# Attention and routed experts on one core: the first pairs' steps in another order, two experts with fewer places

## The chip, the cores and the metric

The kernel runs on 1 core of a Trainium2 chip. The metric is device time in microseconds (us) of one execution, the median over several runs. An execution's own time is a little longer than its span, which reaches from the first to the last instruction of the profiled execution.

## The reference, cut to what matters

Three layers follow one another: attention that is masked by clusters, a gated layer with a causal convolution, and eight experts of which each token visits one.

```python
def _attn_ref(q, k, v, centroids):            # 2 batches, 8 heads, 768 tokens, 64 wide, 16 clusters
    q_assign = np.argmax(np.einsum('bhsd,hcd->bhsc', q_n, c_n), axis=-1)
    k_assign = np.argmax(np.einsum('bhsd,hcd->bhsc', k_n, c_n), axis=-1)
    mask = q_assign[:, :, :, None] == k_assign[:, :, None, :]
    scores = np.where(mask, scale * np.matmul(q, k.transpose(0, 1, 3, 2)), -1000000000.0)
    attn = np.exp(scores - np.max(scores, axis=-1, keepdims=True))
    attn = attn / (np.sum(attn, axis=-1, keepdims=True) + 1e-09)
    return np.matmul(attn, v)
...
def _moe_ref(x, w_val, conv_w, w_out):        # gate: sigmoid of a causal convolution of 5 taps
    return gate * (x @ w_val) @ w_out
...
def _moe2_ref(x, w_gate, w_local, w1, w2):    # 8 experts, 512 -> 1024 -> 512
        for s in range(S):
            fresh_e = int(np.argmax(logits[b, s]))
            e = fresh_e if s == 0 or local_gate[b, s] < 0.5 else prev_e
            prev_e = e
            out[b, s] = softmax(logits[b, s])[e] * (np.maximum(x[b, s] @ w1[e], 0.0) @ w2[e])
```

How many tokens an expert gets depends on the inputs. With the inputs that the reference draws (seed 0), and after 128 tokens of the first batch's largest expert are taken out (the kernel treats them ahead of the rest), the experts hold 306, 260, 220, 203, 132, 104, 102 and 81 tokens, sorted by size. These counts were worked out by running the reference.

## The kernel before, in words

**Attention.** Eight pairs of heads follow one another (`gi` 0 to 7). For each pair, `assign` (step "bg" of the plans) finds the clusters: matmuls `sim`, then on the VectorE (DVE) a transpose `s`, a maximum `amx`, a comparison `eq`, a transpose `et`, then a matmul `bef` and a DVE operation `r` (for the first pair `rb`). `rows` sends the one-hot rows `od` by DMA into the operands `q`, `km` and `oq`. `mx_part` makes score tiles `mx` on TensorE (PE) and reduces each on DVE into `mn`; from these come row maxima, which go back into row 96 of `q`: for the first two pairs by `mx_first` (DVE `mfr`, PE `mt`, ScalarE (ACT) `q<-mt`), later by a DMA. `scores` makes each score tile with two matmuls (`s<-xq,xk`, then `s<-q,km`), ACT takes the exponential into `p`, GpSimd (POOL) sums the `p` into `acc`, and PE multiplies by `v` (`pv`). `prep`, `prep_lo` and `prep_x` split q and k into a high part (`hiq`, `hik`, on ACT) and the remainder (POOL, "qlo" and "klo") and write the operands by DMA. The weights of the next layer (`raww_val`, `raww_out`) are loaded in between and split on DVE in four operations (`split64`: `expw_val`, `topw_val`, ...); the small convolution weights `rawc` take the same way (`small`).

**What sets the order.** Nothing is scheduled by a compiler: every engine runs its instructions in the order in which the program issues them, and all DMAs of the attention are issued by one queue, SyncE's (SP), in its order. `first_pair` writes that order for pair 0 with what the next two pairs need. It counts places n from 0 to 56. At each it issues one `mx` tile, then the steps that the table `FIRST` has at this place, in the table's order, then the row maxima (`LAG`: at place 6i the DVE part of group i is made, its PE part at place 6i + LAG[i]), then as many letters of `ORDER` as `GO` lets through (l: first score matmul of a tile, s: second matmul, exponential and sum, p: `pv`, e: `pv<-oq,eh` and its copy to `xu`). `pair` does the same for pairs 1 to 5 with the table `PLAN`, whose places go from 0 to 35 in each pair, and for the last two with `LATE`, which is not changed.

The PE part of a row maximum is a `mt` matmul behind a DVE reduction:

```python
        nc.vector.tensor_reduce(out=mr, in_=self.mn[gi][:, t0:t0 + n], axis=AX.X, op=ALU.max,
                                negate=True)
        yield
        ps = self.ps_m.tile([128, 512], F32, tag="m", name=f"mt{gi}{h}{a}")
```

**The experts.** The token lists are built on the core, experts sorted by size. `CAPS` holds the places of the first, second, ... largest expert; the tokens beyond them go to blocks of 128 in `beyond`, a loop whose count is read at run time and which runs not at all where every expert fits. In `Ffn.up` (lines 1403 to 1411) an expert with n places up to 256 takes, for each of 32 weight tiles, one matmul `ph<-x,wh` with 2n columns and one `ph<-x,wl` with 256. In `Ffn.down` (line 1447) full tiles of tokens take three matmuls of 512 columns per weight tile. A last tile of 64 or 32 tokens is done otherwise (`rest`, line 1455): matmuls `po<-ws,hr` whose outputs stand beside one another on 64 or 32 partitions, with 256 or 128 columns each. A last tile of 96 is treated as a full one with fewer rows.

Of the kernel before, what the change touches and what calls it, by code (L numbers as in the profile page):

```python
# [34 lines left out]
CAPS = [320, 288, 256, 224, 192, 192, 160, 128]  # L35
# [12 lines left out]
class Attn:  # L48
# [5 lines left out]
    PLAN = (("klo", (22,)), ("acc1", (12,)), ("q", (10,)), ("rows", (21,)), ("qx", (6,)), ("mx", (1, 2, 6, 8, 8, 13, 13, 15, 17, 19, 21, 22, 29, 29, 29, 35)), ("ld", (7,)), ("bg", (3, 5, 5, 7, 7, 15, 15, 24)), ("k", (7,)), ("vs", (11,)), ("vm", (23,)), ("kx", (3,)), ("acc2", (21,)), ("row", (28,)), ("v", (4,)), ("sums", (7, 8, 8, 12, 15, 16, 17, 27, 30, 30)), ("pv", (2, 9, 11, 15, 21, 27, 30, 32, 35)), ("work", (1, 5, 6, 13, 18, 28, 31, 32)), ("qlo", (20,)), ("max", (26,)), ("acc3", (26,)), ("acc4", (31,)), ("sm", (3, 10)))  # L54
    LATE = (("row", (28,)), ("max", (19,)), ("kx", (24,)), ("mx", (1, 3, 4, 8, 8, 10, 12, 13, 13, 15, 20, 21, 21, 23, 23, 23, 23, 29, 29, 29)), ("v", (0,)), ("work", (9, 10, 12, 16, 20, 27, 27)), ("vm", (28,)), ("sums", (6, 11, 12, 16, 21, 24, 25, 27, 28)), ("acc1", (12,)), ("acc4", (35,)), ("pv", (0, 5, 11, 16, 21, 23, 28, 35)), ("acc2", (21,)), ("vs", (13,)), ("qx", (15,)), ("acc3", (22,)), ("sm", (0, 7)))
    MORE = (("mx", (2,)), ("work", (35,)))


    LAG = (7, 10, 14, 12, 28, 6, 13, 13)
    FIRST = (("bg0", (0,)), ("bg0", (0,)), ("q0", (0,)), ("qlo2", (41,)), ("bg0", (0,)), ("bg0", (0,)), ("one1", (16,)), ("bg0", (0,)), ("k2", (32,)), ("bg1", (0,)), ("k0", (0,)), ("klo0", (0,)), ("bg1", (6,)), ("qx0", (1,)), ("bg0", (0,)), ("rows1", (9,)), ("qlo0", (0,)), ("rows0", (17,)), ("v0", (0,)), ("bg1", (0,)), ("bg0", (0,)), ("kx0", (0,)), ("work", (18,)), ("bg1", (0,)), ("rest", (8,)), ("ld2", (10,)), ("klo1", (13,)), ("vs1", (42,)), ("vm1", (52,)), ("qx1", (28,)), ("bg2", (24, 25, 30, 33, 33, 40, 40, 44)), ("bg1", (0,)), ("bg1", (6,)), ("oh0", (0,)), ("v1", (26,)), ("q1", (13,)), ("qlo1", (20,)), ("kx1", (29,)), ("vm0", (16,)), ("vs0", (13,)), ("bg0", (4,)), ("bg1", (0,)), ("klo2", (42,)), ("oh1", (2,)), ("k1", (6,)), ("rows2", (55,)), ("one2", (33,)), ("ld3", (35,)), ("q2", (38,)), ("bg1", (0,)), ("work", (36, 37, 39, 40, 40, 45, 47, 50, 55)))  # L60
    ORDER = "lllsslsslslsllspsllspspplslslsplsplslslselsllssppllslplssppspe"
# [1843 lines left out]
```

## Time and profile before

| | us |
|---|---|
| median of 3 runs | 566.21 |
| the three runs | 566.21, 567.31, 560.71 |
| the profiled execution's own time | 563.89 |
| its span | 562.1 |
| first pair, from the start to pair 1's first scores | about 70 |
| pairs 1 to 7 | about 70 to 285 |
| gated layer and routing | about 285 to 380 |
| experts | about 380 to 562 |

The profile is of one execution. In its views a row gives the start, the duration, the engine, the source line, the operation with output<-input, and in brackets how long the engine stood idle before it and what released it. PEld is the weight load that goes ahead of a matmul, SPq the DMA queue of SyncE. "PEclk" or "granted clock" is TensorE's clock as a share of full speed: 1.00 is 2.4 GHz, 0.50 is 1.2 GHz. Matmuls overlap, so a duration of 0.34 us may stand in a row of matmuls that start every 0.18 us.

### The profile page before, as it was taken

To read this page: it belongs to the slowest core of one execution; us is meant where nothing else is said; L and a number is where in the kernel's file an instruction comes from. 1 tells how busy PE (TensorE), PEld (TensorE's weight loads), DVE (VectorE), ACT (ScalarE), POOL (GpSimd) and SP (SyncE) were. 2 spreads that over 40 slices of the span, in tenths; PEclk is the share of its full clock that TensorE was granted. 3 is DMA by queue.
4 is the path that set the end of the run, shared out by engine and by line. 5 is a ranking of instruction groups with operands and counts; after the bars stand their busy time and mean duration, and the time that the engine had idled before them with its cause. 6 is when DMAs were issued, how large, how long until landed. Compare 5 with 4: busy or idle time off the path is not lost. (4 is left out here: it accounts for less than half of the span.)

```text
span 562.1 us, 9334 instructions
## 1 busy us (share of the span) xinstructions
PE 522.1 (93%) x3328; PEld 387.0 (69%) x3328; DVE 387.3 (69%) x694; ACT 293.8 (52%) x569; POOL 257.9 (46%) x195
## 2 busy tenths in 40 slices
PE   3898979999998999999988999999999999999992
PEld 0564545565655665667678899859898888978892
DVE  4756768787788689767978563646737568479671
ACT  2635354554554565686464241435534548559671
POOL 4475728697897878877931010042013133022011
PEclk9998897999999999999999999999999999999997
DMA  8896284676757452200000038289364887556840
GB/s 203 216 228 184 88 219 127 172 185 169 199 153 174 120 141 81 67 12 0 1 10 0 21 108 305 94 272 342 114 205 162 281 251 232 179 182 211 295 166 14
DMA packets 53180, 86.90 MB, mean 155 GB/s; under 512 B 6313, under 2 KB 30321, under 8 KB 53132
## 3 DMA queue, kind: packets, MB, share of 16 engines
q1 hardware_dynamic: 49996, 78.36, 47.1%
q0 software_dynamic: 3136, 7.92, 4.4%
q8 instruction: 27, 0.44, 0.3%
q14 instruction: 21, 0.17, 0.1%
HBM read 59.65 MB, written 8.62 MB: 121 GB/s over the span
## 5 line engine op out<-in xcount | busy, mean ns | idle before, releaser
L307 DVE TENSOR_REDUCE mn<-mx 128x1 f32<-128x512 f32 (+1 forms) x156 | 94.3, 639 | 29.6 <-PE mx L303 29.4
L398 ACT ACTIVATE p<-s 128x384 f32<-128x384 f32 x168 | 75.4, 488 | 58.5 <-PE s L397 55.3
L1354 DVE TENSOR_TENSOR wl<-ws,wh 128x1024 fp32r<-128x1024 f32 x64 | 77.5, 1222 | 11.0 <-ACT wh L1353 9.8
L476 POOL TENSOR_TENSOR acc<-acc,p 128x768 f32<-128x768 f32 x42 | 84.4, 2033 | 0.5
L1353 ACT ACTIVATE wh<-ws 128x1024 fp32r<-128x1024 f32 x64 | 66.6, 1056 | 6.3 <-DMA ws<-in_w_dram 6.3
L396 PE MATMUL s<-xq,xk 128*128 128x384 f32 x168 | 63.9, 380 | 3.4 <-ACT p L398 3.4
L1480 POOL DMA_INDIRECT out_dram<-o,L x12 | 14.5, 1212 | 112.5 <-ACT o L1479 99.2
L492 PE MATMUL pv<-p,v 128*64 128x384 f32 x336 | 64.8, 507 | 0.0
L303 PE MATMUL mx<-km,q 80*128 80x512 f32 (+1 forms) x192 | 60.7, 387 | 2.3 <-DVE mn L307 1.9
L397 PE MATMUL s<-q,km 97*128 97x384 f32 x168 | 57.4, 342 | 0.0
L1408 PE MATMUL ph<-x,wh 128*128 128x384 f32 (+4 forms) x192 | 56.5, 338 | 0.0
L396 PEld LDWEIGHTS s<-xq,xk 128*128 128x128 f32 x168 | 32.0, 191 | 34.7 <-issue 19.2
L796 DVE SCALAR_TENSOR_TENSOR gp<-xT,cwt,gp 128x767 f32<-128x767 f32 (+3 forms) x32 | 51.5, 1625 | 2.5 <-ACT gp L790 2.1
L1411 PE MATMUL ph<-x,wl 128*128 128x256 f32 x192 | 51.6, 279 | 0.0
L303 PEld LDWEIGHTS mx<-km,q 80*128 80x128 f32 x192 | 37.3, 207 | 15.4 <-DVE mn L307 8.1
L492 PEld LDWEIGHTS pv<-p,v 128*64 128x64 f32 x336 | 20.7, 138 | 27.8 <-issue 27.4
L1447 PE MATMUL po<-wh,hh 128*128 128x512 f32 x96 | 39.0, 407 | 0.0
L1408 PEld LDWEIGHTS ph<-x,wh 128*128 128x128 f32 x192 | 36.1, 188 | 3.2 <-issue 1.0
L1447 PE MATMUL po<-wh,hl 128*128 128x512 f32 x96 | 37.8, 393 | 0.0
L1447 PE MATMUL po<-wl,hh 128*128 128x512 f32 x96 | 37.6, 391 | 0.0
L1411 PEld LDWEIGHTS ph<-x,wl 128*128 128x128 f32 x192 | 36.0, 188 | 0.1
L476 POOL TENSOR_TENSOR acc<-p,p 128x768 f32<-128x768 f32 x14 | 26.2, 1884 | 20.7 <-ACT p L398 20.7
(350 smaller groups left out, 1096.7 us busy)
## 6 DMA issues: line engine op xcount, KB each, us to landing
ws<-in_w_dram SPq DMA_DIRECT2D x72, 512.0 KB
qt<-in_qT_dram SPq DMA_DIRECT2D x8, 384.0 KB
kt<-in_kT_dram SPq DMA_DIRECT2D x8, 384.0 KB
q<-hiq SPq DMA_DIRECT2D x16, 192.0 KB
km<-hik SPq DMA_DIRECT2D x16, 192.0 KB
v<-in_v_dram SPq DMA_DIRECT2D x8, 384.0 KB
xk<-kt SPq DMA_DIRECT2D x16, 192.0 KB
xk<-hik SPq DMA_DIRECT2D x16, 192.0 KB
```

Source lines behind the costliest of these rows:

```text
L303: nc.tensor.matmul(ps[:, n * p:n * p + n], lhsT=q2[0:80, h, t * 128:t * 128 + 128], rhs=km[0:80, h, c:c + n], start=(p == 0), stop=True, s ...
L307: nc.vector.tensor_reduce(out=out, in_=src, axis=AX.X, op=ALU.max)
L396: nc.tensor.matmul(ps, lhsT=kl[:, h, ks], rhs=t1[:, h, hs], start=True, stop=False)
L397: nc.tensor.matmul(ps, lhsT=km[:97, h, ks], rhs=q2[:97, h, hs], start=False, stop=True)
L398: nc.scalar.activation(pt[:, h, hs], ps, AF.Exp, scale=1.0 / D ** 0.5)
L476: eng.tensor_tensor(t[:, h], p(0)[:, h] if first is None else t[:, h], p(j)[:, h], op=ALU.add)
L492: nc.tensor.matmul(self.pvt[64 * h:64 * h + 64, i, :HS], lhsT=v[:, j, 64 * h:64 * h + 64], rhs=pt[:, h, half(i)], start=False, stop=(j == ...
L1353: nc.scalar.activation(hi, t, AF.Copy)
L1354: nc.vector.tensor_tensor(lo, t, f32(hi), op=ALU.subtract)
L1408: nc.tensor.matmul(ps[:, m, :2 * n], lhsT=hi[:, k, ms], rhs=x[:, k, :2 * n], start=st, stop=False, skip_group_check=True)
L1411: nc.tensor.matmul(ps[:, m, :256], lhsT=lo[:, k, ms], rhs=x[:, k, :256], start=False, stop=sp, skip_group_check=True)
L1447: nc.tensor.matmul(self.po[r][i][:m], lhsT=a[:, k, ts], rhs=w[:, q], start=(k == 0 and z == 0), stop=(k == KF - 1 and z == 2))
```

## The change

The tables of the first pair (`LAG`, `FIRST`, `ORDER`, `GO`) and of pairs 1 to 5 (`PLAN`) are written anew, and two numbers of `CAPS` are smaller. The tables' other lines are not shown, since their numbers say nothing to a reader; what they do to the engines' order stands below. The `made` lines only record and assert the order while the program is built and issue nothing.

```diff
-CAPS = [320, 288, 256, 224, 192, 192, 160, 128]
+CAPS = [320, 288, 224, 224, 192, 160, 160, 128]
...
-    LAG = (7, 10, 14, 12, 28, 6, 13, 13)
...
+    LAG = (6, 10, 14, 10, 27, 6, 12, 10)
...
-    ORDER = "lllsslsslslsllspsllspspplslslsplsplslslselsllssppllslplssppspe"
...
+    ORDER = "lllsslsslslsllspsllspspplsllssplsplslslslelslssppllslplssppspe"
...
+        self.made |= {("sim", gi, "q"), ("sim", gi, "k")}
...
     def prep_lo(self, gi, which):
+        assert ("sim", gi, which) in self.made
...
+        self.made.add(("pv", 0, n))
...
-        assert self.t2
+        assert self.t2 and ("pv", 0, NT * h + NT - 1) in self.made
```

The first place is PE, in the middle of the first pair, around the row maximum of pair 1's second group (`mx_5_1`, `mt`). `s_17` to `s_19` are score tiles of pair 0, two matmuls each. Before:

```order
L423 MATMUL s_16_592<-q_0_85,km_88 128x384
L451 MATMUL pv_443<-oq_129,eh_131 64x384 x2
L413 MATMUL s_17_603<-xq_91,xk_93 128x384
L423 MATMUL s_17_603<-q_0_85,km_88 128x384
L413 MATMUL s_18_607<-xq_91,xk_93 128x384
L413 MATMUL s_19_609<-xq_91,xk_93 128x384
L423 MATMUL s_18_607<-q_0_85,km_88 128x384
L303 MATMUL mx_5_1_613<-km_89,q_1_86 128x384
L343 MATMUL mt_628<-identr,mfr_626 128x128 x3
L423 MATMUL s_19_609<-q_0_85,km_88 128x384
```

And of the changed kernel:

```order
L425 MATMUL s_16_592<-q_0_85,km_88 128x384
L415 MATMUL s_17_598<-xq_91,xk_93 128x384
L454 MATMUL pv_443<-oq_129,eh_131 64x384 x2
L305 MATMUL mx_5_1_605<-km_89,q_1_86 128x384
L345 MATMUL mt_620<-identr,mfr_618 128x128 x3
L305 MATMUL mx_6_0_625<-km_89,q_1_86 128x384
L415 MATMUL s_18_631<-xq_91,xk_93 128x384
L425 MATMUL s_17_598<-q_0_85,km_88 128x384
L305 MATMUL mx_6_1_635<-km_89,q_1_86 128x384
L305 MATMUL mx_7_0_642<-km_89,q_1_86 128x384
L415 MATMUL s_19_646<-xq_91,xk_93 128x384
L425 MATMUL s_18_631<-q_0_85,km_88 128x384
```

Four matmuls of the score tiles 17 to 19 that stood ahead of `mx_5_1` and `mt` now stand behind them; on ACT the exponentials of tiles 17 and 18 likewise move behind `q<-mt`, and `hiq` moves from behind tile 19 to ahead of tile 18.

The second place is PE at the end of the first pair. `pv_443<-oq_129,eh_131` is the last reader of `oq_129`, the buffer into which SP writes pair 2's `oq`; `vm` is a small matmul for the mean of v. Before:

```order
L343 MATMUL mt_734<-identr,mfr_685 128x128 x3
L423 MATMUL s_23_697<-q_0_85,km_88 128x384
L441 MATMUL pv_443<-p_4_594,v_202 64x384
L441 MATMUL pv_443<-p_5_689,v_202 64x384
L364 MATMUL vm_744<-vs_682,ones 64x128
L366 MATMUL vm_744<-cnt_279,selg 64x1
L343 MATMUL mt_754<-identr,mfr_539 128x128 x3
L451 MATMUL pv_443<-oq_129,eh_131 64x384 x2
```

And of the changed kernel:

```order
L345 MATMUL mt_734<-identr,mfr_685 128x128 x3
L444 MATMUL pv_443<-p_4_594,v_200 64x384
L444 MATMUL pv_443<-p_5_689,v_200 64x384
L454 MATMUL pv_443<-oq_129,eh_131 64x384 x2
L345 MATMUL mt_748<-identr,mfr_538 128x128 x3
L366 MATMUL vm_753<-vs_683,ones 64x128
L368 MATMUL vm_753<-cnt_279,selg 64x1
```

The last reader of `oq_129` now stands ahead of `vm` and of one `mt`, and `s_23` has gone further up.

The third place is DVE early in pair 1, where the weights `raww_val` are awaited from a DMA; `t_0<-sm` begins the sums of pair 0. Before:

```order
L185 TENSOR_TENSOR eq_832<-s_3_815,amx_830 128x384
L307 TENSOR_REDUCE mn_775<-mx_2_1_845 128x2
L728 TENSOR_SCALAR expw_val_850<-raww_val_834 128x512
L188 STREAM_TRANSPOSE et_860<-eq_832 128x384
L534 STREAM_TRANSPOSE t_0_870<-sm_821 128x384
```

And of the changed kernel:

```order
L186 TENSOR_TENSOR eq_832<-s_3_819,amx_830 128x384
L309 TENSOR_REDUCE mn_775<-mx_2_1_841 128x2
L189 STREAM_TRANSPOSE et_845<-eq_832 128x384
L731 TENSOR_SCALAR expw_val_852<-raww_val_834 128x512
L537 STREAM_TRANSPOSE t_0_866<-sm_821 128x384
```

`et`, which needs no DMA, moves ahead of the operation that waits for one. The same two operations change places in pairs 3 and 4 (there with `raww_out`).

Besides these: on DVE, near the start, `rb` moves ahead of the second pair's `amx`; on SP the loads of pair 2's q and k move ahead of the DMAs of pair 1's `od` rows, and in pairs 1 to 5 two `km` writes move ahead of the q and k loads; on POOL in pairs 1 to 5 the remainder of k moves ahead of the sum over `p_2`; on PE in pairs 1 to 5 one `pv` matmul group and one `mx` tile change places.

## Rows read from the trace of the kernel before

**Rows 1.** The page's first part: busy time by engine.

```profile
PE 522.1 (93%) x3328; PEld 387.0 (69%) x3328; DVE 387.3 (69%) x694; ACT 293.8 (52%) x569; POOL 257.9 (46%) x195
```

**Rows 2.** Windows: length, busy PE, PEld, DVE, ACT, POOL; then clock, DMA share, GB/s.

```profile
50.00:52.00 2.00, 0.08 (x1) 0.00 (x0) 1.75 (x7) 0.76 (x2) 1.08 (x2) 1.00 0.99 336
...
54.00:56.00 2.00, 2.00 (x7) 0.62 (x6) 1.50 (x3) 0.55 (x1) 0.89 (x1) 0.50 0.19 46
...
66.00:68.00 2.00, 1.93 (x11) 0.70 (x10) 1.56 (x4) 0.97 (x2) 1.88 (x2) 1.00 0.00 0
...
86.00:88.00 2.00, 2.00 (x8) 0.47 (x4) 1.91 (x3) 0.06 (x1) 2.00 (x3) 0.50 1.05 246
```

**Rows 3.** Timeline of 47 to 54 us: PE's first long hole and its neighbours.

```profile
49.74 0.34 PE L303 MATMUL mx<-km,q 80*128 80x384 f32 x1
...
51.96 0.15 DVE L338 TENSOR_REDUCE mfr<-mn 128x3 fp32r<-128x9 f32 x1
...
52.26 0.52 PE L343 MATMUL mt<-identr,mfr 128*128 128x128 f32 x3 [2.19 <-DVE mfr L338]
...
53.71 0.83 ACT L261 ACTIVATE hiq<-qt 128x768 fp32r<-128x768 f32 x1
```

**Rows 4.** Timeline of 73 to 83 us: PE's second long hole and what leads to it.

```profile
73.52 0.58 SPq L717 DMA_DIRECT2D raww_val<-in_w_val_dram  x1
...
80.51 0.43 DVE L728 TENSOR_SCALAR expw_val<-raww_val 128x512 uint32<-128x512 uint32 x1 [4.14 <-DMA raww_val<-in_w_val_dram]
80.85 0.57 DVE L188 STREAM_TRANSPOSE et<-eq 128x384 bf16<-128x384 bf16 x1
81.34 0.54 DVE L534 STREAM_TRANSPOSE t<-sm 128x384 f32<-128x384 f32 x1
...
82.66 0.44 PE L396 MATMUL s<-xq,xk 128*128 128x384 f32 x1 [2.68 <-ACT p L398]
```

**Rows 5.** Timeline of PE and SP, 67 to 70 us: what frees `oq`.

```profile
67.54 0.49 PE L441 MATMUL pv<-p,v 128*64 128x384 f32 x1
...
68.43 0.87 PE L451 MATMUL pv<-oq,eh 128*64 128x384 f32 x4
...
69.34 0.78 SPq L253 DMA_DIRECT2D oq<-od  x2
```

**Rows 6.** The waits of SP's queue: us in total, times, longest.

```profile
SPq L253 <- PE pv L451: 6.5, 1, 6.5
```

**Rows 7.** Timeline of 13 to 38 us: DVE's start, SP's od rows, pair 1's first mx.

```profile
13.40 0.55 DVE L182 TENSOR_REDUCE amx<-s 128x24 f32<-128x384 f32 x1
13.87 0.55 DVE L201 SCALAR_TENSOR_TENSOR rb<-bef,et 128x384 bf16<-128x384 f32 x1
...
24.76 0.52 SPq L249 DMA_DIRECT2D q<-od  x1
...
37.41 0.34 PE L303 MATMUL mx<-km,q 80*128 80x384 f32 x1
```

**Rows 8.** ACT's waits for POOL from 100 to 285 us: total, times, longest.

```profile
ACT p L398 <- POOL acc L476: 2.3, 3, 1.6
```

**Rows 9.** Line 1408 by expert (256, 224, 192, 160 places): count, min/median/max ns, starts.

```profile
L1408 PE MATMUL ph<-x,wh x32: 397/397/504, 437.8 to 448.9; 128*128 128x512 f32 x32
...
L1408 PE MATMUL ph<-x,wh x32: 363/365/371, 461.1 to 471.0; 128*128 128x448 f32 x32
...
L1408 PE MATMUL ph<-x,wh x32: 332/332/446, 503.0 to 512.0; 128*128 128x384 f32 x32
...
L1408 PE MATMUL ph<-x,wh x32: 307/310/412, 522.5 to 530.8; 128*128 128x320 f32 x32
```

**Rows 10.** Line 1455, last tiles of 64 and of 32 tokens, one expert each.

```profile
L1455 PE MATMUL po<-ws,hr x32: 379/379/431, 518.9 to 522.2; 128*64 128x256 f32 x32
...
L1455 PE MATMUL po<-ws,hr x64: 272/273/297, 537.1 to 538.8; 128*32 128x128 f32 x64
```

**Rows 11.** Windows of 20 us over the experts, columns as in Rows 2.

```profile
500.00:520.00 20.00, 20.00 (x136) 16.77 (x134) 14.88 (x19) 13.62 (x25) 3.15 (x3) 1.00 0.70 235
```

More of the change, by code (lines that the diff above doesn't have):

```diff
@@ L52 @@
     ENGINES = "svssssss"
-    PLAN = (("klo", (22,)), ("acc1", (12,)), ("q", (10,)), ("rows", (21,)), ("qx", (6,)), ("mx", (1, 2, 6, 8, 8, 13, 13, 15, 17, 19, 21, 22, 29, 29, 29, 35)), ("ld", (7,)), ("bg", (3, 5, 5, 7, 7, 15, 15, 24)), ("k", (7,)), ("vs", (11,)), ("vm", (23,)), ("kx", (3,)), ("acc2", (21,)), ("row", (28,)), ("v", (4,)), ("sums", (7, 8, 8, 12, 15, 16, 17, 27, 30, 30)), ("pv", (2, 9, 11, 15, 21, 27, 30, 32, 35)), ("work", (1, 5, 6, 13, 18, 28, 31, 32)), ("qlo", (20,)), ("max", (26,)), ("acc3", (26,)), ("acc4", (31,)), ("sm", (3, 10)))
+    PLAN = (("klo", (22,)), ("acc1", (12,)), ("q", (10,)), ("rows", (22,)), ("mx", (1, 2, 6, 8, 8, 13, 13, 15, 17, 19, 21, 22, 29, 29, 29, 34)), ("ld", (8,)), ("bg", (3, 5, 5, 6, 7, 15, 15, 30)), ("k", (7,)), ("vs", (11,)), ("vm", (23,)), ("qx", (6,)), ("kx", (2,)), ("acc2", (22,)), ("row", (28,)), ("v", (4,)), ("acc3", (27,)), ("sums", (7, 8, 10, 12, 15, 16, 17, 27, 30, 30)), ("pv", (2, 9, 11, 15, 21, 27, 31, 32, 35)), ("work", (1, 5, 6, 13, 18, 28, 31, 32)), ("qlo", (17,)), ("max", (26,)), ("acc4", (31,)), ("sm", (3, 9)))
@@ L61 @@
-    ORDER = "lllsslsslslsllspsllspspplslslsplsplslslselsllssppllslplssppspe"
-    GO = (7, 9, 12, 13, 14, 15, 17, 17, 17, 17, 17, 19, 19, 22, 22, 22, 22, 22, 24, 25, 25, 26, 26, 26, 28, 28, 29, 29, 30, 30, 31, 31, 33, 33, 34, 35, 35, 35, 35, 35, 35, 35, 35, 35, 35, 35, 36, 39, 41, 41, 42, 42, 42, 42, 42, 42, 42, 44, 44, 49, 51, 52)
+    MORE = (("work", (35,)), ("mx", (2,)))
+    LAG = (6, 10, 14, 10, 27, 6, 12, 10)
+    FIRST = (("bg0", (0,)), ("q0", (0,)), ("qlo2", (41,)), ("bg0", (0,)), ("bg2", (24, 25, 30, 33, 33, 40, 40, 44)), ("bg0", (0,)), ("k2", (32,)), ("one1", (15,)), ("k0", (0,)), ("q1", (13,)), ("v1", (24,)), ("klo0", (0,)), ("bg1", (18,)), ("qx0", (4,)), ("q2", (38,)), ("bg0", (0,)), ("bg0", (0,)), ("qx1", (28,)), ("bg1", (0,)), ("qlo0", (0,)), ("rows0", (19,)), ("v0", (0,)), ("bg0", (0,)), ("bg0", (0,)), ("rest", (7,)), ("klo1", (12,)), ("klo2", (41,)), ("vs1", (42,)), ("vm1", (52,)), ("bg1", (0,)), ("bg1", (6,)), ("bg1", (0,)), ("vs0", (13,)), ("kx1", (28,)), ("oh0", (0,)), ("work", (18,)), ("kx0", (0,)), ("rows1", (12,)), ("qlo1", (21,)), ("bg1", (0,)), ("vm0", (16,)), ("bg0", (5,)), ("bg1", (4,)), ("bg1", (6,)), ("oh1", (2,)), ("k1", (6,)), ("ld2", (10,)), ("rows2", (55,)), ("one2", (31,)), ("ld3", (35,)), ("work", (36, 37, 39, 40, 40, 45, 47, 50, 55)))
@@ L64, in __init__ @@
+    ORDER = "lllsslsslslsllspsllspspplsllssplsplslslslelslssppllslplssppspe"
+    GO = (7, 9, 12, 13, 14, 15, 17, 17, 17, 17, 17, 20, 20, 22, 22, 22, 22, 22, 24, 25, 25, 25, 25, 25, 28, 28, 29, 29, 30, 30, 30, 30, 32, 33, 34, 35, 35, 35, 35, 35, 35, 35, 37, 37, 39, 39, 39, 39, 39, 39, 42, 42, 42, 42, 42, 42, 42, 42, 42, 44, 48, 49)
     def __init__(self, tc, g, xT, ident):
```

2 lines of the change are left out of this document (removed).

## The prediction

> **What bounds the kernel now.** I read the page's busy times first. PE is busy for 93% of the span [rows 1], so the kernel is bound by PE in nearly every stage, and something is gained only where PE gets less to do, where it stands idle, or where its clock is low. Next I read windows of 20 us and then of 2 us for PE's idle time and the granted clock. From 100 us on PE is nearly full at clock 1.00; in the experts it is busy for 20.00 of 20 us [rows 11]. What is lost lies in the first 100 us, in two places that look alike.
>
> Hole A lies near 50 us: PE is busy for 0.08 of 2 us [rows 2]. The timeline shows that `mt` waited 2.19 us for DVE's `mfr`, which came only at 51.96, more than two microseconds after the `mx` tile that it needs [rows 3]: the five little operations of the convolution weights stood on DVE ahead of it. Hole B lies at 80 us: PE waited 2.68 us for an exponential on ACT, ACT for the sums' transpose on DVE, and DVE had waited 4.14 us for the DMA of `raww_val`, issued at 73.52 [rows 4]. After each hole PE's clock is granted at 0.50, that is 1.2 GHz, in three 2 us windows in a row (54 to 60, 84 to 90); one of each three stands in the rows [rows 2].
>
> Why was `raww_val` issued so late? SP's queue stood for 6.5 us at one DMA, `oq<-od` [rows 6], which must not write its buffer before PE's `pv<-oq,eh` has read it. That matmul began at 68.43, the DMA went out at 69.34 [rows 5], and everything behind it on SP, five more DMAs and then `raww_val`, followed. Meanwhile the DMA engines moved nothing: their share is 0.00 from 66 to 68 us [rows 2].
>
> **The change part by part.** The sum is made against the profiled execution, 563.9 us.
>
> *Expert places.* The third expert has 220 tokens and gets 224 places instead of 256, the sixth has 104 and gets 160 instead of 192, so that nothing spills and the loop for the rest stays empty. The 32 `ph<-x,wh` matmuls of the third expert shrink from 512 to 448 columns; the fourth expert already runs with 448. From the first to the last start this takes 11.1 us with 512 and 9.9 us with 448 (the `wl` matmuls between them are alike): 1.2 us less. For the sixth expert 384 columns take 9.0 us and 320 take 8.3: 0.7 us less [rows 9]. The third expert's second tile shrinks from 128 to 96 rows, but its 48 matmuls of 512 columns stay. The sixth expert's last tile shrinks from 64 to 32 tokens: 32 matmul passes from 518.9 to 522.2 and a last 0.4 become 64 passes from 537.1 to 538.8 and a last 0.3, so 3.7 us become 2.0: 1.7 us less [rows 10]. Together 1.2 + 0.7 + 1.7 = 3.6 us, all on the path, since PE is full there [rows 11]. What is late next would be ACT, DVE or the weight loads; but the seventh expert already runs with 160 places, with the shorter stages that come with it. If they do bind, the 1.9 us of the first two terms go and 1.7 stay. I take -3.6, with ends at -3.6 and -1.7.
>
> *Start.* `rb` moves ahead of `amx`, so it may begin at 13.40 rather than 13.87 [rows 7], and the one-hot matmuls, the rows and the first `mx` tile hang on it one after the other: -0.5. In the microseconds that follow, PE runs in step with DVE's reductions, so it could also come to nothing: ends -0.5 and 0. The first `mt` now stands directly behind its `mfr`, and pair 1's `bef` takes the place of the `mx` tile that stood between: the same work in another order, 0. The loads of pair 2's q and k pass the `od` rows of pair 1 on SP. Those went out from 24.76 on, and the first tile that needs them began at 37.41 [rows 7]; the 12 us between them are the cover, so 0.
>
> *Hole A.* The order on DVE is unchanged: `mfr` still stands behind the little operations, and `mt` still directly behind `mx_5_1` on PE. So the hole stays. Four matmuls now follow it instead of leading it, which moves the hole and not the end: 0. It could cost something: ACT now has nothing during the hole, and behind it come `q<-mt`, tile 17, then `hiq` with 0.83 us [rows 3] before tiles 18 and 19, whose `pv` then comes later by that. Ends 0 and +0.8.
>
> *Hole B.* Two things shorten it. First, `pv<-oq,eh` now stands directly behind the last `pv`, which began at 67.54; before, it began at 68.43 [rows 5]. At about 0.1 us from one start to the next this makes some 0.8 us, and SP's stop at `oq`, hence `raww_val`, comes earlier by as much, as the DMA engines were idle [rows 2]. Second, `et`, 0.57 us, runs during DVE's wait instead of behind it [rows 4], so the sums' transpose follows the DMA by 0.57 us less. Together -1.4 of the hole's 2.68 us. If the DMA lands no earlier, -0.6 remains; if all of the hole goes, -2.7. I take -1.4, as both durations stand in rows.
>
> *Pairs 1 to 5.* `et` passes the awaited operation in pairs 3 and 4 as well; PE is nearly full there, so 0, at best -1.1. On POOL the remainder of k passes a sum over `p_2`; what follows on POOL waits for both alike, so only that sum comes later. The sums hold `p` buffers that ACT waits for; these waits come to 2.3 us in all now [rows 8], so 0 with an end at +2.3 if they double. The `km` writes on SP and the `pv` against `mx` on PE are exchanges of neighbours: 0.
>
> *Sum.* -3.6 - 0.5 - 1.4 = -5.5, so 558.4 from the profiled execution. That execution lies 2.3 us below the median of the three runs and amid their spread of 6.6 us. The mean of all four times is 564.5, so I add 0.6 and expect 559.0.
>
> The clock deserves its own look. What the low clock costs can be bounded: six windows of 2 us at half speed are at most 6 us of PE's work, 3 us per stretch; but in the second stretch POOL is busy for 2.00 of 2 us and DVE for 1.91 [rows 2], so a faster PE would wait for them, and the price may be near 0. I keep both stretches in the forecast: no row shows whether a hole of half the length is still followed by one.
>
> The Trainium skill (TensorE: Matmul & The Clock Gate, Part 1: The HAM clock gate) says that the low clock is the resting state which activity releases, that the chip's watch over activity runs on without regard to a kernel's start, so that the same kernel ramps at different points from run to run, and that for modelling the ramp costs less than 1% of a typical span and is not worth fitting. By that rule a layout made for the clock brings next to nothing, and the sum would be the expert places alone. The trace agrees as to size (at most 6 of 562 us); it is one execution and shows nothing of how the stretches move.
>
> **The rivals.**
>
> *The layout is neutral, only the expert places count.* For it: the first pair is a chain of waits in which a gain is often eaten by the next wait, and hole A is untouched. Against it: hole B has one clear cause, and two separate edits shorten it. Time 564.5 - 3.6 = 560.9.
>
> *Hole B no longer costs the clock.* For it: the hole is halved. Against it: POOL and DVE are full behind it [rows 2]. With up to 3 us saved, say 2: 557.0.
>
> *Slower: hole A grows.* Its place is the `mt` of pair 1's second group. With ACT empty during the hole and `hiq` ahead of tiles 18 and 19, PE stops a second time, at the `pv` that reads tile 18, by up to 0.8 us, and the clock stays low for two stretches more at up to 3 us each. Time 559.0 + 6.8 = 565.8, above the mean before. It decides from the point where PE has run out of the `mx` and score matmuls that now stand between `mt` and this `pv`. Against it: there are eight such matmuls, some 1.4 us at full clock at 0.18 us from start to start, and about twice that at half.
>
> *The places don't suffice.* The third expert has four places to spare. If the routing on the chip gave it five tokens more, a block of 128 would run at the end, with all of that expert's weights to load first and nothing else beside it: 2 x 512 x 1024 x 4 bytes, 4.2 MB, at the 235 GB/s of [rows 11] are 18 us before it can finish. Time 559.0 + 18 = 577 and more.
>
> **How the numbers follow.** Forecast 0.50, layout neutral 0.22, clock kept 0.15, hole A grows 0.11, places don't suffice 0.02. The likeliest gives 559.0. Its unknown terms reach from 557 to 562; with the neighbours on either side and the 3 us by which runs of one kernel stray, the range is 554.5 to 565.0. About 2%, some 11 us, can be told from no change. Faster by more than that is below 554.9: only if the clock is kept at both holes, 0.08. Slower by more is above 577.5: 0.03, mostly the spill. Within: 0.89.
>
> **What would show it.** Right: `po<-ws,hr` of the sixth expert in 2.0 us and line 1408's stages in 9.9 and 8.3 us; SP's wait at `oq` shorter; `raww_val` landing about 0.8 us earlier against the exponentials of pair 1; DVE's transpose of the sums right behind `expw_val`; PE's hole near 80 us at about 1.3 us; the hole near 50 us still some 2.2 us. Wrong: if PE's hole B is as long as before, if idle time appears in the sixth or seventh expert, or if low clock shows where there was none.

## The result, and the profile after

| | before | after |
|---|---|---|
| median, runs side by side | 565.97 (12 runs) | 559.40 (12 runs) |
| ratio, 95% interval | | 0.9896 [0.9869, 0.9924] |
| the profiled execution's own time | 563.89 | 558.06 |
| its span | 562.1 | 556.2 |

The ratios leave out runs that lie more than 1.5% above the fastest of their kernel: two of the changed kernel's twelve, and three of the six of the last kernel below.

The changed kernel takes 1.0% less, 4.3 to 7.4 us of 566. By the 2% that count as a difference this is no change, as forecast, and 559.4 stands beside a forecast of 559.0. The forecast's parts did not all come true, though.

PE is still full, with 4.8 us less to do in a span that is 5.9 us shorter. The page's first part of the profile after, beside [rows 1]:

```profile
PE 517.3 (93%) x3360; PEld 384.8 (69%) x3360; DVE 384.6 (69%) x694; ACT 292.2 (53%) x569; POOL 258.7 (47%) x195
```

The experts answer to [rows 9] and [rows 10]. By line, with count, min/median/max ns and the first and last start, the third expert (448 columns) and the sixth (320), and then the sixth's last tile, which now has 32 tokens:

```profile
L1411 PE MATMUL ph<-x,wh x32: 363/365/468, 435.7 to 445.7; 128*128 128x448 f32 x32
...
L1411 PE MATMUL ph<-x,wh x32: 307/310/412, 499.8 to 508.1; 128*128 128x320 f32 x32
...
L1458 PE MATMUL po<-ws,hr x64: 272/273/298, 515.0 to 516.7; 128*32 128x128 f32 x64
```

The stages take 10.0 and 8.3 us where 11.1 and 9.0 stood, and the last tile 2.0 where 3.7 stood. PE stays at 20.00 of 20 us there, so nothing took the place of what went.

The two holes, in 2 us windows of the profile after (columns as in [rows 2]):

```profile
50.00:52.00 2.00, 0.30 (x1) 0.04 (x1) 1.59 (x4) 0.94 (x2) 1.84 (x2) 1.00 0.94 157
52.00:54.00 2.00, 1.19 (x5) 1.22 (x6) 0.65 (x5) 0.48 (x1) 0.00 (x0) 0.76 1.02 398
54.00:56.00 2.00, 2.00 (x7) 1.64 (x6) 0.97 (x3) 1.36 (x3) 0.00 (x0) 0.50 0.23 90
...
86.00:88.00 2.00, 2.00 (x14) 1.20 (x11) 2.00 (x3) 0.00 (x0) 2.00 (x3) 1.00 1.01 302
```

Hole A and the low clock behind it are still there. Behind hole B the clock is 1.00 now, where 0.50 stood. The timeline of the profile after, at the places of [rows 3 to 5]:

```profile
51.02 0.94 DVE L734 SCALAR_TENSOR_TENSOR topc<-rawc,expc 128x20 uint32<-128x20 uint32 x1
...
52.81 0.67 PE L345 MATMUL mt<-identr,mfr 128*128 128x128 f32 x3 [2.51 <-DVE mfr L340]
...
69.76 0.81 PE L454 MATMUL pv<-oq,eh 128*64 128x384 f32 x4
...
70.62 0.78 SPq L254 DMA_DIRECT2D oq<-od  x2
...
74.97 0.49 SPq L720 DMA_DIRECT2D raww_val<-in_w_val_dram  x1
...
81.13 0.43 DVE L731 TENSOR_SCALAR expw_val<-raww_val 128x512 uint32<-128x512 uint32 x1 [1.97 <-DMA raww_val<-in_w_val_dram]
...
81.47 0.58 DVE L537 STREAM_TRANSPOSE t<-sm 128x384 f32<-128x384 f32 x1
...
82.83 0.45 PE L398 MATMUL s<-xq,xk 128*128 128x384 f32 x1 [0.41 <-ACT p L400]
```

Hole A is 2.51 us (2.19 before). Hole B is 0.41 us (2.68 before). The `oq` DMA went out at 70.62 and `raww_val` at 74.97, both more than a microsecond later than before, not 0.8 us earlier, since all of the first pair ends later. Counted from pair 1's first score matmul, though, `raww_val` goes out sooner, 2.47 us behind it instead of 3.62. That matmul before, and then after:

```profile
69.90 0.34 PE L396 MATMUL s<-xq,xk 128*128 128x384 f32 x1
```

```profile
72.50 0.34 PE L398 MATMUL s<-xq,xk 128*128 128x384 f32 x1
```

So hole B is shorter against pair 1's own work, but not in time: PE's wait began at 82.42 instead of 79.98, and ended at 82.83 instead of 82.66.

One profile doesn't settle the size of hole B. The changed kernel's second profile has 1.35 us here, and places alone (below), which has the tables of before, has 1.92 where 2.68 stood. From the issue of the load to the operation that awaited it, it took 7.0 us before, 6.2 after, 7.1 in the second profile, and 6.0 to 7.8 over all profiles in which DVE waited for it. That alone moves the hole by more than the 1.4 us of the forecast.

SP's wait at `oq` is 4.4 us (6.5 in [rows 6]), shorter because SP came to it later, and ACT's waits for POOL from 100 to 285 us are 1.9 us (2.3 in [rows 8]). In the waits by engine they read:

```profile
SPq L254 <- PE pv L454: 4.4, 1, 4.4
...
ACT p L400 <- POOL acc L479: 1.9, 2, 1.6
```

### The profile page after: what moved, and what is told of

Read it like the earlier page. It is cut to its first block, busy times and chain, and to the rows that moved or that the text cites. A ratio compares the mean times of both kernels' runs of the same rounds, so it can differ in the third digit from the quotient of the medians.

```text
span 556.2 us, 9402 instructions
## 1 busy us (share of the span) xinstructions
PE 517.3 (93%) x3360; PEld 384.8 (69%) x3360; DVE 384.6 (69%) x694; ACT 292.2 (53%) x569; POOL 258.7 (47%) x195
## 5 line engine op out<-in xcount | busy, mean ns | idle before, releaser
L1483 POOL DMA_INDIRECT out_dram<-o,L x12 | 13.2, 1100 | 110.1 <-ACT o L1482 96.6
L495 PE MATMUL pv<-p,v 128*64 128x384 f32 x336 | 63.5, 499 | 0.0
L1411 PE MATMUL ph<-x,wh 128*128 128x448 f32 (+3 forms) x192 | 54.6, 329 | 0.0
L799 DVE SCALAR_TENSOR_TENSOR gp<-xT,cwt,gp 128x767 f32<-128x767 f32 (+3 forms) x32 | 49.7, 1569 | 2.5 <-ACT gp L793 2.1
L495 PEld LDWEIGHTS pv<-p,v 128*64 128x64 f32 x336 | 20.4, 136 | 27.7 <-issue 27.7
```

The costliest lines, as they stand in the source:

```text
L495: nc.tensor.matmul(self.pvt[64 * h:64 * h + 64, i, :HS], lhsT=v[:, j, 64 * h:64 * h + 64], rhs=pt[:, h, half(i)], start=False, stop=(j == ...
L1411: nc.tensor.matmul(ps[:, m, :2 * n], lhsT=hi[:, k, ms], rhs=x[:, k, :2 * n], start=st, stop=False, skip_group_check=True)
```

## The experiments

"Low clock" below is the TensorE time that a stretch lost: for each 2 us window, 2 us times one minus the granted clock, added up. Ratios are to the kernel before on the same chip.

### Which part brings the gain

Places alone is the kernel before with the new `CAPS`, and layout alone is the changed kernel with the old:

```diff
-CAPS = [320, 288, 256, 224, 192, 192, 160, 128]
+CAPS = [320, 288, 224, 224, 192, 160, 160, 128]
```

Pairs alone is the kernel before with the changed kernel's table for pairs 1 to 5, first pair alone the kernel before with its tables for the first pair.

**Places alone.** 

> The kernel before with the new places alone (224 and 160). Theory: PE is full in the experts, so all of 3.6 us is gained and it adds to the layout's gain: 3.6 us below before (ratio 0.9936), with the third expert's wh stage at 9.9 us, the sixth's at 8.3 us and its last tile in 2.0 us. Rival (the layout is neutral): this kernel is as fast as the changed one, about 6 us below before (0.989). Rival (ACT, DVE or loads bind): only 1.7 us (0.997).

**Layout alone.** 

> The changed kernel with the old places (256 and 192), so the layout alone. Theory: about 2 us below before (ratio 0.996), hole B near 80 us clearly shorter than 2.68 us. Rival (neutral layout): same as before (1.000). Rival (the clock is kept at hole B in most executions): 3 us or more below before (0.995 or less), no windows at 0.50 near 84 to 90 us.

**Pairs alone.** 

> The kernel before with PLAN and MORE of the changed one alone (pairs 1 to 5); first pair and places as before. Theory: of hole B's shortening only the part of et (0.6 us) comes, so 0 to 1 us below before (ratio 0.998 to 1.000). Rival (what gains is in the pairs): the whole of the layout's gain, 2 us or more.

**First pair alone.** 

> The kernel before with LAG, FIRST, ORDER and GO of the changed one alone (first pair); pairs and places as before. Theory: start (0.5 us) and earlier release of oq (0.8 us) gain 1 to 1.5 us (ratio 0.998). Rival (hole A grows, first pair slower): 0 to 2 us above before, pair 1's first scores later than in before.

| kernel | ratio, 95% interval | experts, us |
|---|---|---|
| places alone | 0.9930 [0.9890, 0.9970] | 382.16 to 547.13: 164.97 |
| layout alone | 0.9983 [0.9951, 1.0015] | 380.82 to 549.27: 168.45 |
| pairs alone | 0.9976 [0.9940, 1.0012] | 380.35 to 548.79: 168.44 |
| first pair alone | 0.9986 [0.9950, 1.0021] | 385.50 to 554.04: 168.54 |
| before | | 384.57 to 553.13: 168.56 |
| the changed kernel | 0.9896 [0.9869, 0.9924] | 382.51 to 547.49: 164.98 |

The last column reaches from ACT's first `hh<-ph` to POOL's last write of the output. It is 168.4 to 168.6 us with the old places and 165.0 with the new: 3.5 to 3.6 us, in each profile. So the places bring some 0.65%, and the time of places alone (0.7%) says the same.

For the layout, layout alone leaves at most 2.8 us, and none is not ruled out; neither half of it alone can be told from the kernel before. The changed kernel against places alone gives -1.9 us, with -4.7 to +0.9 when the two intervals are put together, which doesn't rule out none either. The traces agree with that: the time up to the experts, the first number of the last column, is 380.35 us in pairs alone, 384.57 before and 385.50 in first pair alone, and in the changed kernel's two profiles 382.51 and 386.75, so that one and the same kernel moves by more than its layout is worth.

### What the first pair's holes cost

The changed kernel again is the yardstick. "Small operations earlier" puts the five operations of the convolution weights one place earlier on DVE, ahead of `mn<-mx_5_1`, by the first number of this entry of `FIRST`:

```diff
-("work", (36, 37, 39, 40, 40, 45, 47, 50, 55))
+("work", (35, 37, 39, 40, 40, 45, 47, 50, 55))
```

"Load first" has the load of the weights ahead of the next pair's operand writes on SP, by an entry of `PLAN`, and "both" has both edits:

```diff
-("work", (1, 5, 6, 13, 18, 28, 31, 32))
+("work", (1, 1, 6, 13, 18, 28, 31, 32))
```

**The changed kernel again.** 

> The changed kernel once more, as the yardstick for the three runs beside it. Both theories expect 0.989 to 0.993 of the kernel before, hole A of 2.2 to 2.5 us at mt near 52 us, hole B (PE's wait for the exponential near 82 us) of 0.4 to 0.7 us, experts from the first hh to the last scatter in 165.0 us.

**Small operations earlier.** 

> The changed kernel with the five small operations of the convolution weights one place earlier, ahead of mn<-mx_5_1 instead of between it and mfr on DVE. Theory that PE's holes cost time at full price and clock: mt's wait falls from 2.5 to 0.8 to 1.2 us, pair 1's first scores come 1 to 1.5 us earlier, the 0.50 windows at 54 to 60 shrink or go, and the time falls by 1 to 3 us below the changed kernel's (ratio to before some 0.002 to 0.005 lower). Rival, that the first pair is paced by DVE and the holes are only slack that moves: the wait moves to the mx tiles or the row maxima ahead of or behind it, pair 1's first scores come at the same time within 0.4 us, and the time is the same.

**Load first.** 

> The changed kernel with the load of raww_val issued on SP ahead of pair 1's loads and xk/xq writes, in every one of pairs 1 to 5. Theory that hole B is the load's landing: DVE's wait for raww_val falls from 2.0 to 0 to 1.0 us, the sums' transpose t<-sm of pair 0 comes 0.5 to 1.2 us earlier (near 80.3 to 80.9 instead of 81.5), PE's wait for p falls to nothing, time 0.5 to 1 us lower. Rival, that the hole in the changed kernel is already gone and the rest is paced by PE: pair 1's t<-sm no earlier, time the same within 1 us; and the loads that are passed (v, xk, xq) come later, which would add up to 1 us.

**Both.** 

> Both edits of the two runs before. Theory: the two gains add up, 1.5 to 4 us below the changed kernel (555 to 558 us where it takes 559), with no window at granted clock 0.50 between 50 and 95 us if it is the holes that bring the low clock. Rival: the same time as the changed kernel within 1 us, and the low stretches come all the same or move elsewhere.

| kernel | ratio, 95% interval | `mt` waits | first to second `pv<-oq,eh`, us | low clock, 46 to 66 us |
|---|---|---|---|---|
| before | | 2.19 | 47.96 to 68.43: 20.47 | 3.4 |
| places alone | 0.9930 | 2.18 | 48.84 to 69.25: 20.41 | 3.4 |
| pairs alone | 0.9976 | 2.19 | 49.62 to 70.03: 20.41 | 3.4 |
| changed | 0.9896 | 2.51 | 49.06 to 69.76: 20.70 | 3.4 |
| changed, again | 0.9899 [0.9842, 0.9955] | 2.52 | 50.02 to 70.73: 20.71 | 3.4 |
| layout alone | 0.9983 | 2.52 | 49.78 to 68.98: 19.20 | 1.7 |
| first pair alone | 0.9986 | 2.52 | 50.38 to 70.08: 19.70 | 1.7 |
| load first | 0.9974 [0.9937, 1.0010] | 2.52 | 49.40 to 68.61: 19.21 | 1.7 |
| small earlier | 0.9884 [0.9839, 0.9928] | 1.65 | 50.05 to 68.77: 18.72 | 1.7 |
| both | 0.9891 [0.9832, 0.9950] | 1.63 | 49.61 to 67.85: 18.24 | 1.7 |

The fourth column is the first pair from its first head's `pv<-oq,eh` to its second head's. With the same tables for the first pair and the same low clock it repeats to 0.06 us, but for first pair alone: there a second stretch of low clock begins near 69.4 us, ahead of the second mark, which can account for at most 0.3 of its 0.5 us more. Two things can be read from the column.

First, the price of the clock. The same instructions on PE take 20.70 with 3.4 us lost and 19.20 with 1.7, in two profiles each: nearly all of what the clock takes shows in the time, 1.5 of 1.7 us. The stretch varies where nothing in the first pair was edited.

Second, at 3.4 us lost the old tables take 20.43 us on average and the new 20.70. So the new order of the first pair is the slower one by 0.3 us, although it has less between the two marks: the second mark was moved ahead of a `vm` and an `mt` that take 0.9 us, and the first one behind one more score matmul, about 0.2 us.

Small operations earlier shortens hole A by 0.9 us and the stretch by 0.5 (both: by 1.0) against load first and layout alone with the same low clock. The theory asked for 1 to 3 us in the time. The ratio is 0.001 below the changed kernel's, far inside the intervals.

Load first missed. DVE's wait for `raww_val` went as expected, and the sums' transpose of the first pair came at 78.27 instead of 81.47. But the kernel is slower than the changed one beside it, 0.9974 against 0.9899, with medians of 562.03 and 558.92. The timeline of load first shows where the wait went, to ACT:

```profile
73.81 0.35 SPq L720 DMA_DIRECT2D raww_val<-in_w_val_dram  x1
...
77.96 0.38 DVE L731 TENSOR_SCALAR expw_val<-raww_val 128x512 uint32<-128x512 uint32 x1
...
81.23 0.84 ACT L262 ACTIVATE hik<-kt 128x768 fp32r<-128x768 f32 x1 [3.93 <-DMA xk<-hik]
...
82.70 0.45 PE L398 MATMUL s<-xq,xk 128*128 128x384 f32 x1 [1.43 <-ACT p L400]
```

The load is earlier in SP's order, but not in time: it may not go out before DVE's last split operation has read the weights that it replaces, and so it leaves 2.46 us behind pair 1's first score matmul, as without the edit. SP stands at it meanwhile, 3.5 us instead of 0.4:

```profile
SPq L720 <- DVE expw_val L740: 3.5, 1, 3.5
```

The `xk` writes now stand behind the load on SP; `hik` may not overwrite its buffer before they have read it, and the exponentials queue behind `hik` on ACT. PE's wait at the same matmul became 1.43 us, more than the changed kernel's 0.41, and the low clock came back, in the windows of load first:

```profile
86.00:88.00 2.00, 2.00 (x8) 0.78 (x5) 1.95 (x3) 1.04 (x5) 1.99 (x3) 0.50 1.01 279
```

In pair 1, from the start of the first pair's sums to the start of its own, this costs 33.99 us (78.27 to 112.26) against 29.35 in the changed kernel (81.47 to 110.82), which is more than the 3.2 us won ahead of it. That this is what makes the kernel slower isn't shown, though. "Both" has the same wait (1.49 us), the same low clock and the same stretch of 34.09 us (77.65 to 111.74), and yet it takes the changed kernel's time: its slowest run, 560.41, lies below the fastest of load first, 560.62. The one edit between them, the small operations, isn't told from the changed kernel when it stands by itself. So why load first is slow stays open.

### Can hole A be taken away?

Nothing reads the row that `mt` makes before pair 1. So "mt later" puts it four places later on PE, by one number of `LAG`; the next kernel adds the small operations of above:

```diff
-    LAG = (6, 10, 14, 10, 27, 6, 12, 10)
+    LAG = (6, 10, 14, 10, 27, 10, 12, 10)
```

"Split later" then moves the four DVE operations on the first `raww_val` as well, and "vs earlier" the sum over v:

```diff
-("work", (36, 37, 39, 40, 40, 45, 47, 50, 55))
+("work", (35, 41, 42, 43, 43, 45, 47, 50, 55))
...
-("vs1", (42,))
+("vs1", (39,))
```

**mt later.** 

> The changed kernel with the mt of hole A four places later on PE (LAG of that group 10 instead of 6), behind four mx tiles, the score matmuls of tiles 18 and 19 and bef; nothing reads the row that it makes before pair 1. Theory that hole A costs its full length and brings the low clock: mt waits under 0.3 us, no window at granted clock 0.50 between 50 and 62 us, pair 1's first scores 2 to 4 us earlier counted from the first mx tile (about 53 to 55 us instead of 57 to 58), time 2 to 4 us below the changed kernel's 559 (ratio to before 0.982 to 0.987). Rival, that the small operations on DVE hold up PE anyway: PE waits 1.5 to 2.5 us at one of the mx tiles behind (their buffers are freed by DVE) instead of at mt, the low stretch stays, and the time is the same within 1 us.

**mt later, small operations earlier.** 

> As the run before, and the five small operations one place earlier on DVE. Theory: nothing of the hole is left at mt or at the mx tiles behind it (under 0.5 us in all), no low clock between 50 and 62 us, time 2.5 to 4.5 us below the changed kernel's. Rival: DVE is late either way, a wait of 1 us or more stands elsewhere between 48 and 56 us, and the time is the same within 1 us.

**Split later too.** 

> As the run before (mt four places later, small operations one place earlier), and the four operations on the first raww_val of the first pair two to four places later on DVE (places 41 to 43 instead of 37 to 40), behind the reductions mn of four mx tiles and ahead of vs. Theory, that hole A is DVE's queue standing at a DMA or at the small operations, wherever PE meets it: with nothing awaited in DVE's queue PE's waits between 48 and 60 us are under 1 us in all, no window at granted clock 0.50 between 50 and 66 us, pair 1's first scores 2 to 3 us earlier counted from the first mx tile (54 to 55 us), and the time 2 to 4 us below the changed kernel's (ratio to before 0.982 to 0.987). Rival, that what is won in the first pair is given back at hole B, since the weights' next load waits for the same operations and for the oq write: pair 1's sums (t) start no earlier than 65 us after the first mx tile, hole B grows to 2 us or more with the low clock behind it, and the time is the same within 1 us.

**vs earlier too.** 

> As the run before, and the sum over v (vs, 1.49 us on DVE) three places earlier (39 instead of 42), into the 1.94 us in which DVE waited for PE. Theory: DVE reaches the mx tiles near 66 us some 1.5 us sooner, PE's wait of 1.1 us there and the low clock of 66 to 70 us go, so that no window below 1.00 is left between 46 and 70 us; from the first pv<-oq,eh to the second it takes 16 to 17 us instead of 17.9, and the time falls by 1 to 2.5 us (ratio to before 0.982 to 0.986). Rival: the hole goes somewhere else again (the second raww_val, awaited 2.1 us by DVE near 69 us, or hole B with the low clock behind it), and the time is the same within 1 us.

| kernel | ratio, 95% interval | first to second `pv<-oq,eh`, us | low clock, 46 to 70 us |
|---|---|---|---|
| mt later | 0.9916 [0.9876, 0.9957] | 50.63 to 69.22: 18.59 | 1.7 |
| and small operations earlier | 0.9896 [0.9838, 0.9955] | 48.88 to 69.03: 20.15 | 1.7 |
| and split later | 0.9866 [0.9817, 0.9915] | 51.15 to 69.06: 17.91 | 1.7 |
| and vs earlier | 0.9831 [0.9746, 0.9917] | 48.26 to 66.12: 17.86 | 1.7 |

In the first two, `mt` no longer waits and the hole is there all the same, five microseconds on; the times that their theories asked for did not come. The timeline of mt later:

```profile
56.59 0.43 DVE L731 TENSOR_SCALAR expw_val<-raww_val 128x512 uint32<-128x512 uint32 x1 [1.85 <-DMA raww_val<-in_w_val_dram]
56.93 1.01 DVE L309 TENSOR_REDUCE mn<-mx 128x1 f32<-128x384 f32 x2
57.53 0.32 PE L194 MATMUL bef<-et,before 128*128 128x384 bf16 x1 [1.27 <-DVE mn L309]
```

The next operation in DVE's queue awaits a DMA; two reductions stand behind it, and PE stands behind these. With both edits PE arrives still sooner, DVE waits 3.89 us there instead of 1.85, and the stretch is 20.15 us. That is the rival's answer, one wait further on than it was looked for.

Split later takes the awaited operation away from the front of DVE's queue. Its windows, and after them the waits of PE in its timeline:

```profile
56.00:58.00 2.00, 1.81 (x11) 0.93 (x7) 0.76 (x2) 0.00 (x0) 2.00 (x2) 1.00 1.09 255
58.00:60.00 2.00, 1.98 (x8) 0.97 (x9) 1.78 (x3) 1.52 (x4) 2.00 (x2) 1.00 0.50 124
...
66.00:68.00 2.00, 1.98 (x7) 1.35 (x9) 1.31 (x3) 0.16 (x1) 1.83 (x2) 0.64 0.71 244
```

```profile
53.77 0.44 PE L305 MATMUL mx<-km,q 80*128 80x384 f32 x1 [0.68 <-DVE mn L309]
...
57.85 0.91 PE L305 MATMUL mx<-km,q 80*128 80x384 f32 x2 [0.19 <-DVE mn L309]
...
65.97 1.07 PE L305 MATMUL mx<-km,q 80*128 80x384 f32 x2 [1.08 <-DVE mn L309]
```

Between 46 and 66 us no window is below 1.00, for the first time in all these profiles; a hole of 1.08 us and a stretch of low clock stand at 66 us instead. The stretch of the first pair is 17.91 us, where 19.20 stands with the changed kernel's tables and as much clock lost: 1.3 us less. The next load does wait for the moved operations, as the rival said (SP stands 6.2 us at it), but hole B, where the rival looked for the loss, is 0.18 us. The last kernel was to close the hole at 66 us too and did not: PE waits 1.09 us at the same `mx` tile, since what DVE gained it spent waiting for PE ahead of it (0.52 and 1.94 us).

These two have the lowest ratios of all, 0.9866 and 0.9831, but the second rests on three runs; over all six its median is 560.36 against 564.28 for the kernel before. Their intervals overlap the changed kernel's, so that they beat it isn't shown; both intervals lie below 1.

## Why the prediction was right, and where it was wrong

**Places, -3.6: right, term by term.** 1.1 for the third expert (1.2 foreseen), 0.7 and 1.7 for the sixth; together 3.5 to 3.6 between two marks of the trace, in every profile. Neither ACT, DVE nor the weight loads became late, so the lower end, -1.7, did not come.

**Start, -0.5: it came and had no effect.** The first `mx` tile starts at 15.55 instead of 16.11. Places alone, with the old order, has 15.49, but there DVE's first operation came earlier; counted from that operation it is 6.12 us after, 6.58 before and 6.69 in places alone, so that the gain is real. By the first head's `pv<-oq,eh` it is lost: 49.06 after, 47.96 before. What decides most there is how long PE runs at half pace at the start (last section), which differs from one execution to the next by more than this gain.

**Hole A, 0 with an end at +0.8: this step was too low.** The sentence that failed is that four matmuls behind the hole instead of ahead of it move "the hole and not the end". They now run in the stretch of low clock, in the profile after:

```profile
53.70 0.52 PE L415 MATMUL s<-xq,xk 128*128 128x384 f32 x1
54.02 0.52 PE L425 MATMUL s<-q,km 97*128 97x384 f32 x1
```

At equal low clock the first pair lost 0.3 us where the moved marks should have made it 1.1 us shorter, so the place cost about 1.4 us, above the upper end. Four matmuls that start 0.32 us apart, not 0.18, are some 0.6 of that, by estimate, and 0.3 is the hole itself, 2.51 against 2.19 us; the rest is not placed. The hole is longer because one small DVE operation, `topc`, took 0.94 us. In the profile before it took 0.18, and another of the five 0.60. Either one ends within 0.05 us of POOL's sums into `acc`, at 51.17 before and 51.91 after, as if it had waited for them (last section). Before, then POOL after:

```profile
48.00 3.17 POOL L431 TENSOR_TENSOR acc<-acc,p 128x384 f32<-128x384 f32 x3 [0.76 <-ACT p L425]
...
50.59 0.60 DVE L728 TENSOR_SCALAR expc<-rawc 128x20 uint32<-128x20 uint32 x1
51.23 0.18 DVE L731 SCALAR_TENSOR_TENSOR topc<-rawc,expc 128x20 uint32<-128x20 uint32 x1
```

```profile
48.77 3.14 POOL L433 TENSOR_TENSOR acc<-acc,p 128x384 f32<-128x384 f32 x3 [0.23 <-ACT p L427]
```

The slower rival had this place, but by another mechanism, a second stop of PE at the `pv` that reads tile 18. That stop did not come: behind the hole PE's first listed wait is 0.29 us for DVE, at 60.74, and its first for an exponential 0.18 us, at 62.67. Nor did the clock stay low for two stretches more.

**Hole B, -1.4: right against pair 1's own work, but no gain in time.** Both halves came. `et` ahead of the awaited operation does what was said: the sums' transpose starts 0.34 us behind `expw_val` instead of 0.83. And `raww_val` goes out 2.44 to 2.47 us behind pair 1's first score matmul in every profile with the new tables of the first pair (but for those with the load first), and 3.44 to 3.62 us behind it with the old, so it is earlier by 1.0 to 1.2 us where 0.8 was foreseen. It isn't `oq` alone that holds it now: in the profile after SP stands a last 0.4 us for DVE's split of the weights that the load replaces, a wait that the prediction did not have. What the change from 2.68 to 0.41 us has beyond these halves is chance, as the load itself took 0.8 us less. Over the eight profiles with both new tables, or a variant of those of the first pair, hole B is 0.2 to 2.0 us, 0.9 on average; with both old ones it is 2.68 and 1.92. The step that failed is to book this as time: the first pair comes out longer (hole A), PE reaches the hole 2.4 us later, and the hole's end does not come forward.

**The clock behind hole B.** The forecast kept the low stretch and said that its price might be near 0; the rival without it said 2 us. The clock was kept in six of the eight profiles that have the new table for pairs 1 to 5 and the new tables for the first pair (or a variant of these). In all six it takes 29.3 us from the start of the first pair's sums to the start of pair 1's. With low clock and the same table for pairs 1 to 5 it takes 29.97 (pairs alone, 1.7 us lost), 30.84 (layout alone, 1.7) and 30.53 (mt later with small operations earlier, 3.4), and 30.99 before, with 3.4 us lost and the old order. So the price is 0.6 to 1.5 us, between the forecast's 0 and the rival's 2. Together with the shorter hole this about makes up for what the first pair lost. Pair 1's sums, from the first `mx` tile, come after 96.2 us in the kernel before and 97.1 in places alone, and after 95.3, 97.3 and 96.3 in the changed kernel, its second profile and layout alone; pairs alone has 95.4 and first pair alone 100.5.

**Pairs 1 to 5, 0: nothing shows against it.** Pairs alone is not told from the kernel before. From pair 1's sums to pair 4's it takes 85.77 us before, 86.95 after and 84.92 in pairs alone.

**The sum.** 559.4 lies between the forecast and the rival "layout neutral" (560.9), and the layout's measured worth, -1.0 us with -2.8 to +0.8, holds both the forecast's -1.9 and the rival's 0. So the places are settled and the layout is not: it trades a first pair that is slower for a pair 1 with a shorter hole, which more often keeps its clock. That the two profiles differ by 5.9 us in span, near the sum of -5.5, is luck as far as the layout goes. At pair 4's sums the profile after is ahead by 0.3 us (197.77 against 198.10); another 1.7 us come from one pair of DVE operations in the gated layer, which the change does not touch (below); the experts bring 3.6 and what follows them 0.3.

## What to carry to other kernels

Where every engine runs its own queue in order, a hole belongs to the operation at the front of the queue that is late, not to the instruction that is seen waiting: moving the waiting matmul moved the hole to the next one, moving the load passed the wait to another engine, and only taking the awaited operation out of the front of DVE's queue closed the place, while a hole of 1.1 us opened further on. Price a move at the clock that its new place has, and compare two orders by the time between two marks of the trace at equal clock, since "earlier in the order" is not "earlier in time". When a full engine gets less work, as here in the experts, the rows of a neighbour of the same shape give the gain to a tenth of a microsecond.

## What the runs showed of the hardware that was not expected

**Half pace with a granted clock of 1.00.** In the first 33 to 39 us matmuls of 384 columns start every 0.32 us, not every 0.18, though the windows there say 1.00. 384 columns in 0.32 us are 1.2 columns per nanosecond, which would fit the lower of the two levels; whether the granted clock is wrong there or something else halves the pace isn't shown. A window before, then the timeline of PE before, and then after:

```profile
30.00:32.00 2.00, 2.00 (x8) 1.87 (x7) 0.58 (x2) 1.71 (x4) 1.42 (x2) 1.00 1.05 244
```

```profile
30.46 0.52 PE L413 MATMUL s<-xq,xk 128*128 128x384 f32 x1
30.78 0.52 PE L423 MATMUL s<-q,km 97*128 97x384 f32 x1
...
33.54 0.34 PE L413 MATMUL s<-xq,xk 128*128 128x384 f32 x1
33.72 0.34 PE L423 MATMUL s<-q,km 97*128 97x384 f32 x1
```

```profile
33.48 0.52 PE L415 MATMUL s<-xq,xk 128*128 128x384 f32 x1
33.80 0.52 PE L425 MATMUL s<-q,km 97*128 97x384 f32 x1
...
36.48 0.34 PE L415 MATMUL s<-xq,xk 128*128 128x384 f32 x1
36.66 0.51 PE L305 MATMUL mx<-km,q 80*128 80x384 f32 x2
```

The first pair of starts 0.18 us apart comes at 33.5 us before, 36.5 after, 38.9 in layout alone and 39.5 in first pair alone, and the first head's `pv<-oq,eh` at 47.96, 49.06, 49.78 and 50.38. So most of a spread of 2.4 us ahead of that mark lies here, though not all of it: the changed kernel's second profile has 37.4 and 50.02, layout alone 38.9 and 49.78.

**A DVE operation beside POOL may take four times as long.** The changed kernel's two profiles hold the same instruction, once just ahead of a POOL operation and once just behind its start. DVE and POOL in the profile after, then in its second one:

```profile
116.10 0.46 DVE L731 TENSOR_SCALAR expw_out<-raww_out 128x512 uint32<-128x512 uint32 x1 [0.16 <-POOL acc L479]
116.23 2.02 POOL L271 TENSOR_TENSOR qt<-qt,hiq 128x768 f32<-128x768 f32 x1
```

```profile
118.16 1.82 POOL L271 TENSOR_TENSOR qt<-qt,hiq 128x768 f32<-128x768 f32 x1
118.36 1.91 DVE L731 TENSOR_SCALAR expw_out<-raww_out 128x512 uint32<-128x512 uint32 x1 [0.49 <-DMA raww_out<-in_w_out_dram]
```

It ends 0.3 us after POOL's operation, as if it had waited for it. In that profile PE then waits for DVE and ACT, and pair 2's sums come 32.43 us after pair 1's (112.74 to 145.17) instead of 29.50 (110.82 to 140.32), with the clock at 1.00 throughout. Over all the profiles with the changed table for pairs 1 to 5 this stretch takes 27.7 to 34.0 us; only these two were followed to a cause. The Trainium skill (SBUF — State Buffer, Who interferes with whom) says that DVE and GpSimd share one pair of ports as an exclusive lock, and that the order of issue decides which of the two stands still; these rows agree. Likewise in the gated layer, where DVE's `gp` and POOL's `gl` meet: in the profile before two `gp` operations took 3.78 us beside a `gl` of 1.88, and in the profile after 2.06 beside one of 2.70. Before, then after:

```profile
297.32 3.78 DVE L796 SCALAR_TENSOR_TENSOR gp<-xT,cwt,gp 128x765 f32<-128x765 f32 x2
...
298.41 1.88 POOL L845 TENSOR_TENSOR gl<-gp,gh 128x768 fp32r<-128x768 f32 x1 [9.43 <-ACT gh L844]
```

```profile
296.93 2.06 DVE L799 SCALAR_TENSOR_TENSOR gp<-xT,cwt,gp 128x765 f32<-128x765 f32 x2
...
298.02 2.70 POOL L848 TENSOR_TENSOR gl<-gp,gh 128x768 fp32r<-128x768 f32 x1 [9.43 <-ACT gh L847]
```

These 1.7 us are an accident of timing that places alone, with the same tables, does not have (2.06 us), and that the last kernel above has again (3.76 us). A layout is worth what it is worth only for the timings that it meets.

**A hole is not always followed by the low clock, nor the low clock always led by a hole.** Near 84 us PE waited 1.35 us in the changed kernel's second profile and 1.47 in mt later, and the clock stayed at 1.00; in load first it waited 1.43 us and the clock fell to 0.50. In first pair alone the clock fell near 69.4 us, though PE's last listed waits ahead of it were 0.29 us at 60.75 and 0.18 us at 62.69:

```profile
68.00:70.00 2.00, 1.96 (x9) 1.02 (x10) 2.00 (x5) 0.48 (x1) 1.92 (x3) 0.86 0.00 0
70.00:72.00 2.00, 2.00 (x9) 0.74 (x5) 1.04 (x3) 0.38 (x1) 1.92 (x2) 0.50 0.00 0
```

So it isn't shown that a given hole brings the low clock; what a stretch of it costs, once there, is.
